# A top-32 attention with a routed feed-forward behind it, on one core: three weight loads set behind the loads of the rest's tokens, and the first expert's second product in four pieces over 512 columns of one bank

## The chip, the cores and the metric

The kernel runs on one NeuronCore of a Trainium2 chip. The metric is the device time of one launch in microseconds; a kernel's figure is the median of its runs. The engines are TensorE (PE, with its weight loads as PEld), VectorE (DVE), ScalarE (ACT), GpSimd (POOL) and SyncE (SP), which does little but issue DMAs.

## The reference

`q`, `k`, `v` are float32, 2 x 8 heads x 576 x 64. Each row of scores keeps its 32 largest, the softmax is taken over these alone, and the result is multiplied with `v`. The output, laid out as 1,152 tokens x 512, goes through a layer of 8 experts with one expert per token:

```python
logits = x @ w_gate;  expert_idx = np.argmax(logits, axis=1)
# gate_w: the softmax value of the chosen expert
# a token takes the next free slot of its expert (288 slots each), in the order of the tokens
h = np.maximum(np.einsum('ecd,edf->ecf', disp, w1), 0.0)   # 512 -> 1024
y = np.einsum('ecf,efd->ecd', h, w2)                       # 1024 -> 512
out[i] = gate_w[i] * y[expert_idx[i], pos[i]]
```

## The kernel before, in words

**Attention.** `attention` walks over 36 units, each one tile of 128 tokens and one pair of heads (`L` is the last unit, 35), in a software pipeline written out by hand. Behind every fourth unit a token tile is finished (`T` is the last of nine tiles, 8) and goes through `route` (L493) in numbered stages: transposes of the attention's output, the logits with `wg` (L525), the largest of eight on DVE, a slot number, and at stage 5.5 an indirect DMA from POOL (L559) that scatters the tile's 128 tokens as rows into `xbuf` in DRAM, by expert and slot. For the last two tiles most of these stages run on DVE.

**Experts.** Every product is done in split precision: a weight comes as float32 (`load_w`, L594, four loads of 1 MB for each expert: two of `w1`, two of `w2`), and `split_w` (L606) makes a half-precision part of it on ACT (L612) and the remainder on DVE (L618); three products of 16-bit parts replace one in float32. The experts are taken in an order that is picked from running counts. From the first picked expert the first 128 tokens (called `a`) are computed inside the attention's last units, from the second one the first 128 tokens (`b`) in the attention's tail. What those two experts have left, 64 + 64 tokens, is "the rest" (`r`): `load_rest` (L644) reads them from `xbuf` with two transposing DMAs (L648), which have to wait until the last tile's scatter has landed, and `ffn_rest` (L763) computes them, its first product at L773 and its second at L761. Then `experts` runs the six other experts from `ffn` (L819), the next one's weights being split meanwhile. The sixteen-bit tokens of expert 2 and 3 come with `load_x` (L632).

**What sets the order here.** All these DMAs except the scatters are issued by SP, in program order: SP waits at the first one whose buffer or data isn't ready, and all later ones stand behind it. The scatters are issued by POOL on a queue of its own. Buffers come from rotating pools; expert 3's weights go to four buffers (`raw`) that exist from the attention's end on. PSUM has eight banks; `tail_p` (L482) names four of them `TAIL_P[0]` to `TAIL_P[3]` for the tail, `bank1` (L83) hands out two others (`pT`) in turn, which the transposed probabilities use too.

**The tail, and the lines that the change touches.** The second product for `a` is cut into four quarters of 128 output columns (`quarter`, L722), each of 24 matmuls (L757) into a `pT` bank, followed by its own copy on ACT (L720); the quarters stand between the last units' steps, and behind the fourth POOL scatters the 128 finished rows to `out` (L677). Then `b`'s first product (L657), the scatter of the last tile, `check` and `count` (a one-column matmul, counts and ranks, L1003 and L1019), and `b`'s second product (L757, with all 512 columns). On SP stand, in this order: the second half of expert 2's `w2` and both halves of expert 3's `w1` (three loads), `load_rest`, expert 2's tokens, both halves of expert 3's `w2`, expert 3's tokens.

Of the kernel before, what the change touches and what calls it, by code (L numbers as in the profile page):

```python
# [34 lines left out]
def kernel(  # L35
# [47 lines left out]
    def bank1():  # L83
        if ("pt", 0) in P:
            return P["pt", 0].tile([128, 512], FT, name="pT", bufs=2)
        return P["p3", 0].tile([128, 9, 128], FT, name="p3", bufs=1).rearrange("p a b -> p (a b)")[:, :512]

    def bank4():
        return bank1().rearrange("p (c t) -> p c t", c=4)
# [618 lines left out]
        nc.gpsimd.tensor_scalar(hh, Q["r"], 1.0, 0.0, op0=OP.mult, op1=OP.add)  # L708
        nc.gpsimd.tensor_tensor(out=hl, in0=Q["r"], in1=hh, op=OP.subtract)

    def quarter_y(c, a):
        if a == 0:
            Q["p"] = bank4()
        for k in (0, 1) if a == 0 else (2, 3):
            small_y("a", 0, Q["p"][:, 0], slice(128 * c, 128 * c + 128), k < 2, k % 2)

    def quarter_out(c):
        if c == 0:
            Q["y"] = work.tile([128, Dm], FT, name="y", tag="nat", bufs=4)
        nc.scalar.activation(Q["y"][:, 128 * c:128 * c + 128], Q["p"][:, 0], AF.Copy, scale=XE["a"][:, 0, 0:1])  # L720

    def quarter(c):  # L722
        quarter_y(c, 0)
        quarter_y(c, 1)
        quarter_out(c)

    def quarter_scatter():
        scatter_y(Q["y"], XE["a"][:, 0, 1:2])

    def small_h(x, e, *fs, first=None):  # L730
        for f in fs:
            g, a = divmod(f, 4)
            if a == 0:
                PA[x, g] = first if first is not None else bank().rearrange("p (c t) -> p c t", c=4) if BANKS else \
                    bank4()
            h_of(PA[x, g][:, a], e, f, x)
# [15 lines left out]
    def small_y(x, e, o, cols, high, g):  # L752
        for i in range(4 * g, 4 * g + 4):
            for lo in range(1 + high):
                fl = dict(start=(high and i == 0 and lo == 0), stop=(not high and i == KF - 1))
                if x != "r":
                    nc.tensor.matmul(o, HA[x][1 - high][:, i], weight(e, 1, lo)(i, cols), **fl)  # L757
                    continue
                for j in range(2):
                    s = slice(64 * j, 64 * j + 64)  # L760
                    nc.tensor.matmul(o[s], HA[x][1 - high][:, i, s], weight(j, 1, lo)(i, cols), **fl)  # L761
# [237 lines left out]

    def check(step):  # L1000
        if step == 1:
            pf = bank1()
            nc.tensor.matmul(pf[:1, 0:1], onesb[:, 0:1], fl[:, 0:1], start=True, stop=True)  # L1003
            nc.vector.tensor_copy(flags[:, 0:1], pf[:1, 0:1])
            return
        ck = work.tile([128, 4, NT * H], FT, name="ck", tag="hl2", bufs=2)
        nc.vector.tensor_scalar(ck[:, 0], CNT, 0.5, None, op0=OP.mult)
        nc.vector.tensor_copy(ci, ck[:, 0])
        nc.vector.tensor_copy(ck[:, 1], ci)
        nc.vector.tensor_tensor(out=ck[:, 2], in0=ck[:, 0], in1=ck[:, 1], op=OP.not_equal)  # L1010
        nc.vector.scalar_tensor_tensor(ck[:, 1], CNT, float(2 * TOPK - S), ck[:, 2], op0=OP.is_lt, op1=OP.add)
        nc.vector.scalar_tensor_tensor(ck[:, 2], CNT, float(2 * TOPK - S + 14), ck[:, 1], op0=OP.is_gt, op1=OP.add)
        nc.vector.tensor_reduce(out=ck[:, 3, 0:1], in_=ck[:, 2], axis=mybir.AxisListType.X, op=OP.max)
        nc.vector.tensor_copy(fl[:, 0:1], ck[:, 3, 0:1])


    def count():
        pc = bank1()
        nc.tensor.matmul(pc[:1, :E], onesb[:, 0:1], OHS, start=True, stop=True)  # L1019
        m = work.tile([1, 4, E, E], FT, name="cm", tag="hl2", bufs=2)  # L1020
        g = m[:, 3]
        n, key, rank = g[:, 0], g[:, 1], g[:, 2]
        down, across = [1, E, E], (lambda a: a[:, None, :].to_broadcast([1, E, E]))
        nc.vector.tensor_copy(n, pc[:1, :E])
        nc.vector.scalar_tensor_tensor(key, n, float(E), last, op0=OP.mult, op1=OP.add)
        nc.vector.tensor_tensor(out=m[:, 0], in0=across(key), in1=key[:, :, None].to_broadcast(down), op=OP.is_gt)
        nc.vector.tensor_reduce(out=rank, in_=m[:, 0], axis=mybir.AxisListType.X, op=OP.add)
        nc.vector.tensor_tensor(out=m[:, 1], in0=across(rank), in1=places[:, :, None].to_broadcast(down),
                                op=OP.is_equal)
        nc.vector.tensor_tensor(out=m[:, 2], in0=m[:, 1], in1=across(e_f[:1]), op=OP.mult)  # L1030
        nc.vector.tensor_reduce(out=g[:, 3], in_=m[:, 2], axis=mybir.AxisListType.X, op=OP.add)
        nc.vector.tensor_copy(order, g[:, 3])
        nc.vector.tensor_tensor(out=m[:, 0], in0=m[:, 1], in1=across(n), op=OP.mult)
        nc.vector.tensor_reduce(out=key, in_=m[:, 0], axis=mybir.AxisListType.X, op=OP.add)
        nc.vector.tensor_tensor(out=n, in0=key, in1=room, op=OP.is_gt)
        nc.vector.tensor_reduce(out=rank[:, 0:1], in_=n, axis=mybir.AxisListType.X, op=OP.max)
        nc.vector.tensor_copy(many, rank[:, 0:1])
        nc.vector.tensor_tensor(out=bad, in0=rank[:, 0:1], in1=flags, op=OP.add)
# [8 lines left out]
    def attention(side, early, late, mid, pads, act, pool, end):  # L1047
# [110 lines left out]
            bound(L, st)  # L1158
        sign(L)
        run(rt(T - 2, 4))  # L1160
        quarter(0)
        values(L - 2)
        seq(select, L - 1, steps=(0, 1, 2, 3))
        run(rt(T - 2, 5))
# [19 lines left out]
        load_w(2, 1, 0)  # L1184
        for st in range(2, 9):
            pick(3, st)
        quarter(1)
        probs(L, 0, 1, 2)
        values(L - 1)
        run(rt(T - 1, 3, 3.5))  # L1190
# [1 line left out]
            split_w(1, 1, 1, half, nc.scalar, 2)  # L1192
        run(rt(T - 1, 4, 5, 5.5))
        split_w(1, 1, 1, 0, nc.vector, 1)
        quarter(2)
        run(rt(T, 0, 0.5))
        values(L)
        run(rt(T, 1))
        quarter(3)
        quarter_scatter()  # L1200
        seq(normalise, L, steps=(0, 1, 2))
        split_w(1, 1, 1, 1, nc.vector, 1)
        load_w(2, 1, 1)
        close_pool("att")
        open_pool("exp")
        for g in range(2):
            load_w(3, 0, g, True)
        run(rt(T, 0.1))
        small_h("b", 1, 0, first=TAIL_P[2].rearrange("p (c t) -> p c t", c=4))
        run(rt(T, 0.6, 1.1, 1.5))  # L1210
        small_h("b", 1, 1)
        run(rt(T, 2.1, 2.2, 3))
        small_h("b", 1, 2)
        run(rt(T, 3.5, 4, 5, 5.5))
        for f in range(3, KF):
            small_h("b", 1, f)
            if f % 4 == 3:
                small_high("b", f // 4)
        check(0)
        check(1)  # L1220
        count()
        load_rest([nc.sync.value_load(row[:, e:e + 1], min_val=0, max_val=(E - 1) * cap + 128) for e in range(2)])
        load_x(2, 0, SIZES[2])
        for g in range(2):
            load_w(3, 1, g, True)
        load_x(3, 0, SIZES[3])
        small_low("b", 0)
        small_low("b", 1)
        split(2, 0, 2)
        split(2, 0, 1)  # L1230
        split(2, 1, 2)
        o = bank1()
        for high in (True, False):
            for g in range(2):
                small_y("b", 1, o, slice(0, Dm), high, g)
# [180 lines left out]
```

## Time and profile before

| | us |
|---|---|
| median of 3 runs (lowest, highest) | 365.16 (362.47, 365.77) |
| the profiled execution | 364.38 |
| its span, first to last instruction | 362.6 |
| PE busy in it | 319.3 (88%) |
| DVE, ACT, POOL busy | 305.5, 283.2, 238.9 |
| DMA traffic | 60.25 MB, mean 166 GB/s |
| mean granted TensorE clock | 0.978 of 2.4 GHz |

Engine times are sums over all instructions, and overlap; a PE that is busy is not a PE at its peak. The attention fills the first 248 us or so, the six experts from `ffn` the last 85, and between them lies the stretch that the change rearranges.

### The profile page before, as it was taken

To read this page: it belongs to the slowest core of one execution; us is meant where nothing else is said; L and a number is where in the kernel's file an instruction comes from. 1 tells how busy PE (TensorE), PEld (TensorE's weight loads), DVE (VectorE), ACT (ScalarE), POOL (GpSimd) and SP (SyncE) were. 2 spreads that over 40 slices of the span, in tenths; PEclk is the share of its full clock that TensorE was granted. 3 is DMA by queue.
4 is the path that set the end of the run, shared out by engine and by line. 5 is a ranking of instruction groups with operands and counts; after the bars stand their busy time and mean duration, and the time that the engine had idled before them with its cause. 6 is when DMAs were issued, how large, how long until landed. Compare 5 with 4: busy or idle time off the path is not lost. (4 is left out here: it accounts for less than half of the span.)

```text
span 362.6 us, 9845 instructions
## 1 busy us (share of the span) xinstructions
PE 319.3 (88%) x3378; PEld 264.9 (73%) x3381; DVE 305.5 (84%) x1605; ACT 283.2 (78%) x498; POOL 238.9 (66%) x274
## 2 busy tenths in 40 slices
PE   6747888898888988989789999989789999999991
PEld 3535776787777876868588888989346999996681
DVE  5879999999999999999999996596626859799940
ACT  5879999999989999899899996762336847786820
POOL 3967979699894998999999989974011010219421
PEclk9888999999999999999899999999989999999998
DMA  9749897964485800000304524527579999997100
GB/s 168 129 106 208 201 217 211 221 150 101 100 281 193 309 3 31 4 0 32 116 3 129 200 82 125 216 98 247 214 213 343 316 392 308 322 381 169 59 25 24
DMA packets 69922, 60.25 MB, mean 166 GB/s; under 512 B 52070, under 2 KB 52070, under 8 KB 69864
## 3 DMA queue, kind: packets, MB, share of 16 engines
q1 hardware_dynamic: 67719, 54.79, 54.7%
q0 software_dynamic: 1616, 4.73, 3.6%
q8 instruction: 28, 0.46, 0.5%
q14 instruction: 31, 0.25, 0.2%
q10 hardware_dynamic: 528, 0.02, 0.1%
HBM read 40.66 MB, written 12.09 MB: 145 GB/s over the span
## 5 line engine op out<-in xcount | busy, mean ns | idle before, releaser
L310 DVE MAX8 un<-s 128x8 f32<-128x72 f32 (+2 forms) x576 | 102.1, 225 | 1.8 <-PE s L292 1.8
L372 POOL TENSOR_TENSOR z<-sm,sg 128x576 f32<-128x576 f32 x71 | 89.4, 1280 | 12.7 <-ACT sg L365 10.6
L677 POOL DMA_INDIRECT out_dram<-y,xp x12 | 24.4, 2033 | 82.8 <-DVE y L853 40.2
L453 PEld LDWEIGHTS pV<-vm,pT 128*128 128x128 f32 (+1 forms) x640 | 72.2, 183 | 6.9 <-issue 3.6
L453 PE MATMUL pV<-vm,pT 128*128 128x65 f32 (+1 forms) x640 | 73.3, 263 | 0.0
L618 DVE TENSOR_TENSOR ws<-wr,ws 128x1024 bf16<-128x1024 f32 x52 | 61.2, 1226 | 2.6 <-ACT ws L612 2.5
L356 ACT ACTIVATE sm<-s,mx 128x576 f32<-128x576 f32 (+2 forms) x108 | 54.7, 580 | 7.3 <-DVE mx L313 7.0
L365 ACT ACTIVATE sg<-sm,mx 128x576 bf16<-128x576 f32 x72 | 55.2, 770 | 5.8 <-POOL z L372 2.7
L292 PE MATMUL s<-qk 128*128 128x512 f16 (+3 forms) x320 | 45.4, 300 | 9.8 <-ACT sm L356 9.8
L428 PE MATMUL p<-ident,sm 128*128 128x128 f32 x252 | 48.3, 281 | 6.0 <-ACT xT L522 5.5
L409 ACT ACTIVATE pen<-sm,nk 128x576 bf16<-128x576 f32 x71 | 51.5, 775 | 1.8 <-DVE nk L400 1.3
L396 DVE MAX8 z<-z 128x8 f32<-128x576 f32 x72 | 51.0, 748 | 1.9 <-POOL z L372 1.9
L612 ACT ACTIVATE ws<-wr 128x2048 f16<-128x2048 f32 (+1 forms) x26 | 47.6, 1840 | 5.7 <-issue 4.4
L657 PEld LDWEIGHTS <-ws 128*128 128x128 f16 (+1 forms) x768 | 48.8, 98 | 0.9 <-issue 0.4
L429 PE MATMUL p<-identB,pen 128*128 128x128 bf16 x252 | 44.6, 220 | 3.5 <-ACT pen L409 3.4
L428 PEld LDWEIGHTS p<-ident,sm 128*128 128x128 f32 x252 | 36.1, 143 | 10.3 <-ACT xT L522 6.8
L429 PEld LDWEIGHTS <-pen 128*128 128x128 bf16 x324 | 33.5, 105 | 6.9 <-ACT pen L409 6.0
L292 PEld LDWEIGHTS <-qk 128*128 128x128 f16 (+1 forms) x320 | 20.8, 107 | 21.7 <-issue 13.8
L430 ACT ACTIVATE pT<-p 128x1152 f32<-128x1152 f32 x28 | 31.9, 1140 | 0.0
L618 POOL TENSOR_TENSOR ws<-wr,ws 128x1024 bf16<-128x1024 f32 x12 | 25.6, 2131 | 0.0
L838 PEld LDWEIGHTS <-ws 128*128 128x128 f16 (+1 forms) x288 | 21.3, 98 | 0.0
L657 PE MATMUL bk<-xe,ws 128*128 128x128 f16 (+7 forms) x312 | 21.1, 227 | 0.0
(276 smaller groups left out, 622.4 us busy)
## 6 DMA issues: line engine op xcount, KB each, us to landing
wr<-in_moe_w_dram SPq DMA_DIRECT2D x32, 1024.0 KB, 6.1
xbuf<-zero SPq DMA_DIRECT2D x6, 771.0 KB, 5.8
qnat<-in_q_dram SPq DMA_DIRECT2D x16, 144.0 KB, 3.5
knat<-in_k_dram SPq DMA_DIRECT2D x16, 144.0 KB, 3.4
out_dram<-zero SPq DMA_DIRECT2D x3, 768.0 KB, 4.6
vm<-in_v_dram SPq DMA_DIRECT2D x16, 128.0 KB, 3.1
qk<-qk SPq DMA_DIRECT2D x14, 144.0 KB, 2.4
vt<-in_v_dram SPq DMA_DIRECT2D x4, 64.0 KB, 4.6
```

Of the source, the lines that this page charges most:

```text
L292: nc.tensor.matmul(PS[u][a][row:row + n, o:o + w], QK[b][2 * i][:, h, s:s + n], QK[b][1][:, h, c:c + w], start=(i == 0), stop=(i == 1))
L310: nc.vector.max(out=un[:, j, i], in_=segment(u, j, i))
L356: nc.scalar.activation(SM[u][:, j, o], i, AF.Identity, bias=VAL[u][0][:, 0, j:j + 1], scale=-1.0)
L365: nc.scalar.activation(SG[u][j], SM[u][:, j], AF.Sign, bias=VAL[u][0][:, 2, j:j + 1], scale=-(1.0 - 2.0 ** -20), accum_out=CNT[:, c:c + 1])
L372: engs[j].tensor_tensor(out=Z[u][:, j], in0=SM[u][:, j], in1=SG[u][j], op=OP.mult)
L396: nc.vector.max(out=z8[:, step - 1], in_=Z[u][:, step - 1])
L409: eng.activation(o, x, AF.Relu, bias=n)
L428: nc.tensor.matmul(pt[:, i], sm[:, cs], ident, start=True, stop=False, is_transpose=True)
L429: nc.tensor.matmul(pt[:, i], pen[:, cs], identB, start=False, stop=True)
L453: nc.tensor.matmul(PV[t][row:row + n, h0 + half], PT[u][:, 5 * half + c, row:row + n], VM[b][:, c, p, half], start=False, stop=(half == 1 ...
L618: eng.tensor_tensor(out=w[:, 1].bitcast(BF)[:, s], in0=r[:, s], in1=w[:, 0, s], op=OP.subtract)
L657: nc.tensor.matmul(o, a(i), c(i), start=(i == 0 and m == 0), stop=(i == k - 1 and m == 2))
```

## The change

Two things. First, on SP three loads of 1 MB (the second half of expert 2's `w2`, both halves of expert 3's `w1`) move from ahead of `load_rest` to behind it, and `load_rest` itself is written ahead of `check` and `count`. Second, `a`'s second product is cut by its terms instead of its columns: the first two pieces hold 8 matmuls each (the half-precision part of the hidden values times both parts of the weights), the last two 4 each, all over 512 columns in one bank, `TAIL_P[2]`; one copy on ACT follows instead of four, and the scatter of those rows is issued behind that of the last tile. For this `b`'s first product now writes `pT` banks, `check` and `count` `TAIL_P[0]`, and `b`'s second product `TAIL_P[3]` (the bank that prints as `ex`).

```diff
@@ -708,21 +708,12 @@
         nc.gpsimd.tensor_scalar(hh, Q["r"], 1.0, 0.0, op0=OP.mult, op1=OP.add)
         nc.gpsimd.tensor_tensor(out=hl, in0=Q["r"], in1=hh, op=OP.subtract)
 
-    def quarter_y(c, a):
-        if a == 0:
-            Q["p"] = bank4()
-        for k in (0, 1) if a == 0 else (2, 3):
-            small_y("a", 0, Q["p"][:, 0], slice(128 * c, 128 * c + 128), k < 2, k % 2)
-
-    def quarter_out(c):
-        if c == 0:
-            Q["y"] = work.tile([128, Dm], FT, name="y", tag="nat", bufs=4)
-        nc.scalar.activation(Q["y"][:, 128 * c:128 * c + 128], Q["p"][:, 0], AF.Copy, scale=XE["a"][:, 0, 0:1])
-
-    def quarter(c):
-        quarter_y(c, 0)
-        quarter_y(c, 1)
-        quarter_out(c)
+    def quarter_y(c):
+        small_y("a", 0, TAIL_P[2], slice(0, Dm), c < 2, c % 2)
+
+    def quarter_out():
+        Q["y"] = work.tile([128, Dm], FT, name="y", tag="nat", bufs=4)
+        nc.scalar.activation(Q["y"], TAIL_P[2], AF.Copy, scale=XE["a"][:, 0, 0:1])
 
     def quarter_scatter():
         scatter_y(Q["y"], XE["a"][:, 0, 1:2])
@@ -999,7 +990,7 @@
 
     def check(step):
         if step == 1:
-            pf = bank1()
+            pf = TAIL_P[0]
             nc.tensor.matmul(pf[:1, 0:1], onesb[:, 0:1], fl[:, 0:1], start=True, stop=True)
             nc.vector.tensor_copy(flags[:, 0:1], pf[:1, 0:1])
             return
@@ -1015,7 +1006,7 @@
 
 
     def count():
-        pc = bank1()
+        pc = TAIL_P[0] if TAIL_P else bank1()
         nc.tensor.matmul(pc[:1, :E], onesb[:, 0:1], OHS, start=True, stop=True)
         m = work.tile([1, 4, E, E], FT, name="cm", tag="hl2", bufs=2)
         g = m[:, 3]
@@ -1158,7 +1149,7 @@
             bound(L, st)
         sign(L)
         run(rt(T - 2, 4))
-        quarter(0)
+        quarter_y(0)
         values(L - 2)
         seq(select, L - 1, steps=(0, 1, 2, 3))
         run(rt(T - 2, 5))
@@ -1184,7 +1175,7 @@
         load_w(2, 1, 0)
         for st in range(2, 9):
             pick(3, st)
-        quarter(1)
+        quarter_y(1)
         probs(L, 0, 1, 2)
         values(L - 1)
         run(rt(T - 1, 3, 3.5))
@@ -1192,44 +1183,43 @@
             split_w(1, 1, 1, half, nc.scalar, 2)
         run(rt(T - 1, 4, 5, 5.5))
         split_w(1, 1, 1, 0, nc.vector, 1)
-        quarter(2)
+        quarter_y(2)
         run(rt(T, 0, 0.5))
         values(L)
         run(rt(T, 1))
-        quarter(3)
-        quarter_scatter()
+        quarter_y(3)
+        quarter_out()
         seq(normalise, L, steps=(0, 1, 2))
         split_w(1, 1, 1, 1, nc.vector, 1)
-        load_w(2, 1, 1)
         close_pool("att")
         open_pool("exp")
-        for g in range(2):
-            load_w(3, 0, g, True)
         run(rt(T, 0.1))
-        small_h("b", 1, 0, first=TAIL_P[2].rearrange("p (c t) -> p c t", c=4))
+        small_h("b", 1, 0)
         run(rt(T, 0.6, 1.1, 1.5))
         small_h("b", 1, 1)
         run(rt(T, 2.1, 2.2, 3))
         small_h("b", 1, 2)
         run(rt(T, 3.5, 4, 5, 5.5))
+        quarter_scatter()
         for f in range(3, KF):
             small_h("b", 1, f)
             if f % 4 == 3:
                 small_high("b", f // 4)
+        load_rest([nc.sync.value_load(row[:, e:e + 1], min_val=0, max_val=(E - 1) * cap + 128) for e in range(2)])
+        load_w(2, 1, 1)
+        load_x(2, 0, SIZES[2])
+        for g in range(4):
+            load_w(3, g // 2, g % 2, True)
+        load_x(3, 0, SIZES[3])
         check(0)
         check(1)
         count()
-        load_rest([nc.sync.value_load(row[:, e:e + 1], min_val=0, max_val=(E - 1) * cap + 128) for e in range(2)])
-        load_x(2, 0, SIZES[2])
-        for g in range(2):
-            load_w(3, 1, g, True)
-        load_x(3, 0, SIZES[3])
         small_low("b", 0)
         small_low("b", 1)
         split(2, 0, 2)
         split(2, 0, 1)
         split(2, 1, 2)
-        o = bank1()
+        o = TAIL_P[3]
         for high in (True, False):
             for g in range(2):
                 small_y("b", 1, o, slice(0, Dm), high, g)
```

The queue of SP around `load_rest` (`wr` is a weight piece, `xe` and `xp` tokens and their scales; the address computations between the rows are left out). Before:

```order
L603 DMA wr_4979<-in_moe_w2_dram 128x4x512
L603 DMA wr_4985<-in_moe_w1_dram 128x2x1024
L603 DMA wr_4987<-in_moe_w1_dram 128x2x1024
L1222 TENSOR_LOAD row_146
L648 DMA_TRANSPOSE xe_5164<-xbuf 128x8x64
L651 DMA xp_5165<-xbuf 64x2
L640 DMA_TRANSPOSE xe_5170<-xbuf 128x8x192
L642 DMA xp_5171<-xbuf 96x2x2
L603 DMA wr_5174<-in_moe_w2_dram 128x4x512
L603 DMA wr_5176<-in_moe_w2_dram 128x4x512
L640 DMA_TRANSPOSE xe_5178<-xbuf 128x8x176
```

Now:

```order
L1208 TENSOR_LOAD row_146
L648 DMA_TRANSPOSE xe_5051<-xbuf 128x8x64
L651 DMA xp_5052<-xbuf 64x2
L603 DMA wr_5057<-in_moe_w2_dram 128x4x512
L640 DMA_TRANSPOSE xe_5059<-xbuf 128x8x192
L642 DMA xp_5060<-xbuf 96x2x2
L603 DMA wr_5063<-in_moe_w1_dram 128x2x1024
L603 DMA wr_5065<-in_moe_w1_dram 128x2x1024
L603 DMA wr_5067<-in_moe_w2_dram 128x4x512
L603 DMA wr_5069<-in_moe_w2_dram 128x4x512
L640 DMA_TRANSPOSE xe_5071<-xbuf 128x8x176
```

The three loads that stood first (4979, 4985, 4987) are 5057, 5063 and 5065 now: one behind the rest's tokens, two behind expert 2's tokens. The rows of L648 and L651 stand twice each.

ACT at the end of the attention (`y` is the result for `a`, `xT` the last tile's transposed output, in two halves). Before:

```order
L612 ACTIVATE ws<-wr 128x1024 x2
L720 ACTIVATE y<-pT,xp 128x128
L522 ACTIVATE xT<-bk 128x256
L720 ACTIVATE y<-pT,xp 128x128
L522 ACTIVATE xT<-bk 128x256
L531 ACTIVATE xs<-xr 128x512
```

Now:

```order
L612 ACTIVATE ws<-wr 128x1024 x2
L522 ACTIVATE xT<-bk 128x256
L716 ACTIVATE y<-bk,xp 128x512
L522 ACTIVATE xT<-bk 128x256
L531 ACTIVATE xs<-xr 128x512
```

The third and fourth copy of 128 columns (the first two stand further ahead) give way to one of 512, in the fourth one's place.

## Rows read from the trace of the kernel before

**Rows 1.** Waits of PE from 225 us on: total us, times, longest.
```profile
PE bk L773 <- DMA xe<-xbuf: 2.3, 2, 1.4
PE pV L450 <- ACT pT L430: 0.7, 1, 0.7
```
**Rows 2.** Timeline of PE: start, us, line, out<-in, count [idle before <-releaser].
```profile
246.86 1.05 PE L757 MATMUL pT<-ws,hh 128*128 128x128 f16 x16
...
248.19 0.39 PE L516 MATMUL bk<-ident,xr 128*128 128x128 f32 x2
...
255.76 3.62 PE L757 MATMUL pT<-ws,hh 128*128 128x512 f16 x15 [0.34 <-DVE cm L1024]
259.21 1.89 PE L757 MATMUL pT<-ws,hl 128*128 128x512 f16 x8
...
262.46 0.40 PE L773 MATMUL bk<-ws,xe 128*64 128x512 f16 x1 [1.36 <-DMA xe<-xbuf]
263.83 7.05 PE L773 MATMUL bk<-ws,xe 128*64 128x512 f16 x47 [0.97 <-DMA xe<-xbuf]
270.82 0.66 PE L780 MATMUL bk<-ident,hs 128*128 128x128 f32 x4
...
274.44 1.92 PE L761 MATMUL pT<-ws,hh 128*64 128x512 f16 x16 [0.37 <-ACT hh L782]
276.19 1.89 PE L761 MATMUL pT<-ws,hl 128*64 128x512 f16 x16
```
**Rows 3.** Busy time by stretch: window, us, engines busy, granted clock, DMA share, GB/s.
```profile
255.00:257.00 2.00, 1.37 (x7) 0.61 (x7) 1.48 (x8) 2.00 (x2) 0.00 (x0) 1.00 1.00 410
264.76:268.17 3.41, 3.41 (x20) 1.42 (x18) 1.29 (x2) 0.00 (x0) 1.01 (x1) 0.50 0.73 150
266.00:333.00 67.00, 66.48 (x808) 57.96 (x805) 50.30 (x57) 45.01 (x49) 13.00 (x6) 0.98 1.07 329
332.00:334.00 2.00, 2.00 (x16) 1.06 (x15) 2.00 (x3) 0.10 (x1) 2.00 (x1) 1.00 0.18 32
```
**Rows 4.** Timeline of SP and its longest wait.
```profile
246.63 1.66 SPq L603 DMA_DIRECT2D wr<-in_moe_w_dram  x3
259.71 2.57 SPq L648 DMA_TRANSPOSE xe<-xbuf  x2
...
264.36 1.44 SPq L640 DMA_TRANSPOSE xe<-xbuf  x1
...
SPq L648 <- DMA xbuf<-xs,ru: 10.0, 1, 10.0
```
**Rows 5.** Timeline of POOL: scatters of the first expert's rows and the last tile's tokens.
```profile
249.04 0.98 POOL L677 DMA_INDIRECT out_dram<-y,xp  x1 [2.82 <-ACT xT L522]
...
252.96 1.00 POOL L559 DMA_INDIRECT xbuf<-xs,ru  x1 [1.66 <-DVE ck L1009]
```
**Rows 6.** Landing of the eight earlier L559 scatters: issue to landing.
```profile
DMA to landing us min/median/max: 3.0/3.1/3.4
```
**Rows 7.** DMA queues (packets, MB, share): 249.04 to 252.9, 253 to 256.9, 257 to 259.
```profile
q1 hardware_dynamic: 580, 1.42, 95.2%
...
q1 hardware_dynamic: 340, 1.33, 83.9%
q0 software_dynamic: 80, 0.26, 16.6%
...
q0 software_dynamic: 79, 0.26, 33.4%
```
**Rows 8.** Timeline of ACT: copies at the attention's end, and the last expert's weights.
```profile
248.40 0.37 ACT L720 ACTIVATE y<-pT,xp 128x128 f32<-128x128 f32 x1 [3.30 <-PE pT L757]
...
263.56 0.67 ACT L1237 ACTIVATE y<-pT,xp 128x512 f32<-128x512 f32 x1
...
340.84 1.92 ACT L612 ACTIVATE ws<-wr 128x2048 f16<-128x2048 f32 x1
344.67 0.69 ACT L815 ACTIVATE y<-bk,xp 128x512 f32<-128x512 f32 x1 [1.92 <-PE bk L757]
```

## The prediction

> **What bounds the kernel now.** I read the waits of PE first. From 225 us to the end PE's longest wait by far is that of the rest's first product (L773) for its tokens, 2.3 us in two pieces [rows 1]; the last row of that view in time is the 0.37 us ahead of 274.44 [rows 2], and behind it PE doesn't wait once. So what this change can give lies before that point, and a microsecond that PE gains there counts to the end unless something else has become late. The timeline of PE [rows 2] shows the place: `b`'s second product ends at about 261.1, the first matmul on the rest starts at 262.46, the second at 263.83, and the 48 last until 270.82. The stretches [rows 3] show what follows from the pause: from 264.76 to 268.17 the granted clock is 0.50 (1.2 instead of 2.4 GHz), where it was 1.00 ahead of the pause. The wait, then, is paid twice, and the stretch from 261.1 to 270.82, 9.7 us, holds 48 matmuls that need far less.
>
> Why the tokens are late is seen on three queues. SP issues the three weight loads at 246.63 to 248.29 and then waits 10.0 us for the last scatter [rows 4]. POOL issues that scatter at 252.96 [rows 5], and SP comes through at 259.71: 6.75 us, where the eight earlier ones landed after 3.0 to 3.4 [rows 6]. In between the three loads pass: the hardware queue holds the DMA engines for 95% of the time until 252.9, and the software queue moves nothing, though the scatter of `a`'s rows was issued at 249.04. That one's 80 packets go through by 256.9, the tokens' 79 only from 257 to 259 [rows 5, 7]. I read that as scatters kept back by the weights.
>
> **The tokens.** With the three loads behind `load_rest`, nothing of weight size is under way when the scatter is issued. I take the median landing of the eight, 3.1 us [rows 6]; the bounds are 3.0 and the 6.75 of now. That brings SP's transposes to 3.65 us earlier by itself.
>
> The trace says that the scatters were kept back until the loads were nearly through [rows 7]. The Trainium skill ("DMA: Bandwidth & Descriptors", Queues, rings and completion order) says otherwise: each DMA engine takes turns between the queues it has work for, packet by packet. By that rule the tokens lose little to the loads, and the whole change would bring 1.4 us instead of the 5.5 of the sum; the packets of rows 7 speak against it.
>
> **The four pieces.** A quarter now takes 248.19 - 246.86 = 1.33 us for 24 matmuls of 128 columns; the other three look the same. Over 512 columns with the same kind of weights, 16 take 259.21 - 255.76 = 3.45 us, 0.216 each [rows 2]. So the pieces take 8 x 0.216 = 1.72, 1.72, 0.86 and 0.86 us: the first two 0.39 longer, the last two 0.47 shorter. The first two lie ahead of the place where PE waits 0.7 us for ACT's exponentials at L450 [rows 1]; I cost them at nothing, with that wait as their cover (without it, 0.8 us). The last two lie behind it, in the chain from the last unit to the last tile's route, so PE reaches the last transposes (L516, 248.19) 0.94 us sooner. On ACT the copy of `a` still stands ahead of the tile's `xT`: 0.67 us for 512 columns (L1237) [rows 8] in place of the fourth quarter's 0.37, so 0.30 of it is given back; the three other copies go, where ACT had room. Net 0.64. All that comes then hangs on this chain: logits, slots, the scatter of the tokens, `b`'s first product.
>
> **Other banks and moves.** `count` no longer shares a bank with `b`'s second product, and the wait of 0.34 us for DVE at 255.76 goes [rows 2]. That product then starts at 255.76 - 0.64 - 0.34 = 254.8 and ends at about 260.1. The scatter of `a`'s rows moves behind that of the tokens on POOL; it costs POOL 0.98 us [rows 5] at a time when POOL has nothing else, and nobody reads `out`. `load_rest` ahead of `check` changes nothing on SP, since neither issues there.
>
> **The sum.** Scatter at 252.96 - 0.64 = 252.3; landing 3.1 later; SP's first transpose at 255.5 instead of 259.71, 4.2 us sooner; the second half of the tokens is usable 263.83 - 259.71 = 4.12 us behind that, at 259.6, ahead of PE's 260.1. Both waits go, by half a microsecond only. Without the pause the clock should stay: 16 such matmuls take 276.19 - 274.44 = 1.75 us at full clock [rows 2], so 48 take 5.25 and end at 265.35 instead of 270.82. That is 5.5 us: 1.0 ahead of the product, 2.3 of waits, and the remaining 2.2 mostly the 3.4 us at half clock (1.7) and the matmul that ran alone. 364.38 (the profiled execution) becomes 358.9; it stands 0.8 below the median of the runs, so **the forecast is 365.16 - 5.5 = 359.7 us**.
>
> **What is late next: the weights.** From 266 to 333 the DMA engines have no rest (share 1.07, which counts overlapping packets, 329 GB/s); only at 332 to 334 does it fall to 0.18 [rows 3]. Three loads of 1.05 MB that used to pass before 259 now enter this stretch. At 410 GB/s each costs 2.6 us, at 329 it costs 3.2, so 7.7 to 9.6. The stretch starts sooner: the first of them stands where expert 2's tokens were issued, 264.36 [rows 4], less 4.2. All loads behind come 3.5 to 5.4 us later while PE wants them 5.5 sooner: 9.0 to 10.9 us of slack are used. The last weight piece is in by some 332.4 (the share of the last row) and is taken by ACT at 340.84, and ACT idles 1.92 us behind it [rows 8]: 8.4 + 1.9 = 10.3. That covers all but the far end, so I cost this at nothing, and at 0.6 us for the upper bound. Earlier pieces have more room.
>
> **Rivals.** (1) *The queues share fairly*, and the scatter is slow for another reason. The tokens' 79 packets are 5 for each of 16 engines; a weight packet let in ahead of each holds 1.33 MB / 340 = 3.9 KB [rows 7] and takes 0.15 us at a sixteenth of 410 GB/s: 0.8 us in all. The second half then arrives at 263.83 - 0.64 - 0.8 = 262.4, PE waits 2.3 us as before and the clock falls: 365.16 - 1.4 = 363.8. For it speaks only that both queues did move packets between 253 and 256.9. Chance 0.10.
>
> (2) *The tokens come sooner, but the clock falls all the same*, or a wait of a microsecond is left (the margin is 0.5). Half of 3.41 us is 1.7: 361.4. The clock was at 1.00 from 255 to 257, and the pause is all that lies between. Chance 0.15.
>
> (3) *Slower: the weights become the bound.* The place is ACT's split of the last expert's fourth piece (340.84), the price each microsecond by which it lands behind 340.84 + 1.92. If the scatter stays at 6.75 us, the head start is 0.64 instead of 4.2; with loads at 329 GB/s the last piece lands at 332.4 + 9.6 - 0.6 = 341.4, still covered. It decides from 342.8 on: 1.4 us more, which three more loads in a saturated queue can cost, as can a second pause of PE with its 1.7 us of half clock. I take 3 us beyond cover and pause: 368. Against it stands that the loads fit in by rate. Chance 0.05.
>
> (4) *No effect*, the moved loads being late on another path that takes back all that is won: 365. Chance 0.03.
>
> **The numbers.** The forecast has 0.67; with the runs' spread (362.47 to 365.77) its own range is 358 to 361.3. A change of 1% (3.65 us) is about what a measurement of this kernel tells from none. Faster by more than that, below 361.5: all of the forecast and half of rival 2, 0.74. Within: the other half, rivals 1 and 4 and part of 3, 0.21. Slower: 0.05. The range goes from 357.6 to 363.2: it takes in rival 2 and leaves out 1, 3 and 4.
>
> **What will show it.** In the new profile the last L559 lands some 3 us after its issue; SP's L648 starts near 255.5; no wait for `xe` at the rest's first product, whose 48 matmuls take 5.2 to 5.4 us at a granted clock of 1.00; the copy of `a` is one of about 0.67 us. The forecast is wrong if SP's wait for the scatter lasts as long with the engines idle, if a stretch at half clock is left, or if ACT's L612 of the last experts waits for a load.

## The result, and the profile after

The change made the kernel faster by 1.3%: 359.93 us (359.45 to 360.11) against 364.94 us (362.47 to 365.77) in the same series, ratio 0.9874 [0.9839, 0.9909]. A second series of both gave 360.21 and 365.04 us, 0.9874 [0.9828, 0.9919]. (One execution of 1,734.61 us is left out of the first figures; none like it came again in six more runs of the same kernel, and its cause is open.) The forecast was 359.7 us. The profiled execution took 359.45 us with a span of 357.7, where it was 364.38 and 362.6.

Line numbers behind the change are lower than before, most by 9: `b`'s second product is L748, the rest's first product L764 and its transposes L771, the second product of an expert's 128 tokens L748 too; the copy of `a`, inside the change, is L716. The experiments that start from the kernel before keep its numbers (in e5 those behind the added line are one higher).

I read the scatter first, on POOL's timeline of the changed kernel, with its landing from the DMA issues (line, operation, count, median us to landing):

```profile
252.17 1.01 POOL L559 DMA_INDIRECT xbuf<-xs,ru  x1 [2.17 <-DVE ck L1000]
253.49 0.98 POOL L677 DMA_INDIRECT out_dram<-y,xp  x1 [0.30 <-issue]
```
```profile
xbuf<-xs,ru POOLq DMA_INDIRECT x1, 3.1
```

It is issued 0.79 us sooner than before and lands after 3.1 us where it took 6.75 [rows 4, 5]. SP's timeline answers to it:

```profile
255.30 2.56 SPq L648 DMA_TRANSPOSE xe<-xbuf  x2
...
259.59 0.41 SPq L603 DMA_DIRECT2D wr<-in_moe_w_dram  x1
260.20 2.30 SPq L640 DMA_TRANSPOSE xe<-xbuf  x1
...
263.73 3.01 SPq L603 DMA_DIRECT2D wr<-in_moe_w_dram  x4
```

SP passes at 255.30 instead of 259.71 [rows 4], and the three loads follow behind. Next PE's timeline, at the same places as in [rows 2], and one place near the end:

```profile
246.23 1.02 PE L748 MATMUL bk<-ws,hl 128*128 128x512 f16 x4
247.09 0.38 PE L516 MATMUL bk<-ident,xr 128*128 128x128 f32 x2
...
254.57 3.63 PE L748 MATMUL ex<-ws,hh 128*128 128x512 f16 x16
258.07 1.90 PE L748 MATMUL ex<-ws,hl 128*128 128x512 f16 x8
259.91 5.37 PE L764 MATMUL bk<-ws,xe 128*64 128x512 f16 x48
265.21 0.66 PE L771 MATMUL bk<-ident,hs 128*128 128x128 f32 x4
...
336.06 1.90 PE L748 MATMUL bk<-ws,hh 128*128 128x512 f16 x8 [0.73 <-ACT hh L732]
```

The last transposes of the attention come at 247.09 instead of 248.19. The rest's 48 matmuls stand in one row with no idle time ahead of it, and end at 265.2 where they ended at 270.82: 5.61 us won here. The stretches (columns as in [rows 3]) show the clock:

```profile
264.76:268.17 3.41, 3.28 (x30) 1.68 (x26) 1.20 (x2) 2.83 (x3) 0.23 (x1) 1.00 1.14 179
261.00:333.00 72.00, 71.53 (x906) 63.15 (x903) 57.68 (x62) 51.78 (x55) 20.47 (x8) 1.00 1.08 339
332.00:334.00 2.00, 2.00 (x30) 1.64 (x28) 1.70 (x2) 1.77 (x3) 1.70 (x2) 1.00 1.04 384
```

The granted clock is 1.00 where it was 0.50. The third row shows the price: at 332 to 334 the DMA share is 1.04 and not 0.18, so the weights now arrive some microseconds later, and PE wants them sooner. The waits of PE from 225 us on, and ACT's timeline, show where that bites:

```profile
PE pV L450 <- DVE xr L469: 1.0, 1, 1.0
PE bk L748 <- ACT hh L732: 0.7, 1, 0.7
PE pV L450 <- ACT pT L430: 0.7, 1, 0.7
```
```profile
247.29 0.69 ACT L716 ACTIVATE y<-bk,xp 128x512 f32<-128x512 f32 x1 [2.81 <-PE bk L748]
...
330.98 1.91 ACT L612 ACTIVATE ws<-wr 128x2048 f16<-128x2048 f32 x1 [0.26 <-DMA wr<-in_moe_w_dram]
333.61 1.91 ACT L612 ACTIVATE ws<-wr 128x2048 f16<-128x2048 f32 x1 [0.23 <-DMA wr<-in_moe_w_dram]
335.42 0.58 ACT L732 ACTIVATE hh<-pV 128x512 f16<-128x512 f32 x1
336.87 1.91 ACT L612 ACTIVATE ws<-wr 128x2048 f16<-128x2048 f32 x1 [0.86 <-DMA wr<-in_moe_w_dram]
339.72 0.69 ACT L806 ACTIVATE y<-bk,xp 128x512 f32<-128x512 f32 x1 [0.94 <-PE bk L748]
```

Of the last expert's four weight pieces ACT waits for three. The third one's split ends at 335.5, the `hh` (hidden values) that stand behind it on ACT come late, and PE idles 0.73 us at 336.06. The fourth piece is the latest, by 0.86 us, yet costs PE nothing: behind its split ACT idles 0.94 us until PE is done. The two ends meet: 5.61 - 0.73 = 4.88 us, and the span is 4.9 shorter.

### The profile page after: what moved, and what is told of

The parts are those of the page before. It is cut to its first block, busy times and chain, and to the rows that moved or that the text cites. A ratio compares the mean times of both kernels' runs of the same rounds, so it can differ in the third digit from the quotient of the medians.

```text
span 357.7 us, 9700 instructions
## 1 busy us (share of the span) xinstructions
PE 315.1 (88%) x3309; PEld 259.9 (73%) x3309; DVE 305.5 (85%) x1605; ACT 282.5 (79%) x495; POOL 239.5 (67%) x274
## 5 line engine op out<-in xcount | busy, mean ns | idle before, releaser
L372 POOL TENSOR_TENSOR z<-sm,sg 128x576 f32<-128x576 f32 x71 | 89.4, 1279 | 13.1 <-ACT sg L365 10.9
L453 PEld LDWEIGHTS pV<-vm,pT 128*128 128x128 f32 (+1 forms) x640 | 71.3, 181 | 6.7 <-issue 3.3
L453 PE MATMUL pV<-vm,pT 128*128 128x65 f32 (+1 forms) x640 | 72.4, 261 | 0.0
L292 PE MATMUL s<-qk 128*128 128x512 f16 (+3 forms) x320 | 43.4, 292 | 8.8 <-ACT sm L356 8.8
L657 PE MATMUL pT<-xe,ws 128*128 128x128 f16 (+2 forms) x336 | 21.4, 221 | 0.4 <-ACT pen L409 0.4
```

Source lines behind the costliest of these rows:

```text
L292: nc.tensor.matmul(PS[u][a][row:row + n, o:o + w], QK[b][2 * i][:, h, s:s + n], QK[b][1][:, h, c:c + w], start=(i == 0), stop=(i == 1))
L372: engs[j].tensor_tensor(out=Z[u][:, j], in0=SM[u][:, j], in1=SG[u][j], op=OP.mult)
L453: nc.tensor.matmul(PV[t][row:row + n, h0 + half], PT[u][:, 5 * half + c, row:row + n], VM[b][:, c, p, half], start=False, stop=(half == 1 ...
L657: nc.tensor.matmul(o, a(i), c(i), start=(i == 0 and m == 0), stop=(i == k - 1 and m == 2))
```

## The experiments

All kernels of one series share their runs of the kernel before; its median was 365.04 in the first series (the first four kernels), 364.85 in the second, 363.7 in the third. "Ahead" counts the 1 MB loads that stand ahead of `load_rest` on SP, "order" says whether the scatter of `a`'s rows is issued behind that of the tokens, "lands" is the tokens' scatter from issue to landing. A wait marked PEld is that of a weight load in the middle of the 48 matmuls for the second half of the tokens; it isn't among PE's own waits, but makes the 48 take longer.

| | ahead | order | pieces | lands | PE's wait for `xe` | the 48 matmuls | us | ratio to before |
|---|---|---|---|---|---|---|---|---|
| before | 3 | no | no | 6.75 | 2.3 | 0.40 + 7.05 | 365.0 | 1 |
| after_again | 0 | yes | yes | 3.1 | none | 5.37 | 360.21 | 0.9874 [0.9828, 0.9919] |
| e1_loads_only | 0 | no | no | 4.2 | 0.2 (PEld) | 5.67 | 363.09 | 0.9957 [0.9913, 1.0001] |
| e2_pieces_only | 3 | yes | yes | 6.1 | 2.0 | 0.40 + 7.05 | 364.0 | 0.9962 [0.9932, 0.9992] |
| e3_one_ahead | 1 | yes | yes | 3.0 | none | 5.37 | 359.46 | 0.9853 [0.9808, 0.9898] |
| e4_two_ahead | 2 | yes | yes | 4.2 | 0.4 (PEld) | 5.90 | 359.65 | 0.9878 [0.9833, 0.9924] |
| e5_warm_in_pause | 3 | no | no | 6.9 | filled, 0.2 (PEld) | 5.66 | 363.05 | 0.9972 [0.9942, 1.0001] |
| e6_one_ahead_no_pieces | 1 | no | no | 4.5 | 0.4 (PEld) | 5.87 | 360.19 | 0.9896 [0.9851, 0.9942] |
| e7_scatter_order_only | 3 | yes | no | 6.3 | 1.8 | 0.40 + 5.37 | 363.3 | 0.998 [0.9943, 1.0016] |
| e8_five_ahead | 5 | yes | yes | 7.4 | 6.0 | 8.53 | 368.38 | 1.0126 [1.0084, 1.0167] |
| e9_no_pieces_scatter_behind | 1 | yes | no | 3.8 | none | 5.37 | 360.23 | 0.9904 [0.9864, 0.9943] |

**The changed kernel once more.** Expected:

> The changed kernel once more, beside the others of this chip. Theory (the three loads kept the scatter of the last tokens back, and PE's pause brought half clock): 359.9 us again, the rest's first product without a wait, and a wait of 0.7 us at the last expert but one (L748 for hh) because its successor's weights land late. One earlier execution of six took 1,734.6 us; if that belongs to the kernel it comes again in some execution here, if it was the chip's it does not.

Measured 360.21, with the 0.7 us wait of PE for `hh` again.

**The loads alone.** The kernel before, and on SP:

```diff
-        load_w(2, 1, 1)
...
-        for g in range(2):
-            load_w(3, 0, g, True)
...
+        load_rest([...])
+        load_w(2, 1, 1)
+        load_x(2, 0, SIZES[2])
+        for g in range(4):
+            load_w(3, g // 2, g % 2, True)
+        load_x(3, 0, SIZES[3])
         check(0)
         check(1)
         count()
-        load_rest([...])
-        load_x(2, 0, SIZES[2])
-        for g in range(2):
-            load_w(3, 1, g, True)
-        load_x(3, 0, SIZES[3])
```

> The three loads behind load_rest, the quarters and the banks as before. Theory: the scatter (issued near 253.0) lands in 3.0 to 3.4 us, SP's transposes start near 256.2 instead of 259.7, the second half is usable near 260.3, ahead of PE's 261.1, the clock stays at 1.00 and the 48 matmuls take 5.3 us: 4.4 us less ahead of the experts, some 0.2 of it lost to late weights, 360.7. Rival (the queues share the engines fairly, the gain comes from the pieces): the scatter still takes over 6 us, both waits stay, 364.9.

Measured 363.09, with an interval that just reaches 1 and runs that spread from 360.60 to 367.96. PE's timeline, at the rest and near the end, and SP's at the four loads behind:

```profile
261.03 5.67 PE L773 MATMUL bk<-ws,xe 128*64 128x512 f16 x48
...
339.10 1.90 PE L757 MATMUL bk<-ws,hh 128*128 128x512 f16 x8 [2.11 <-ACT hh L741]
```
```profile
266.00 2.31 SPq L603 DMA_DIRECT2D wr<-in_moe_w_dram  x4
```

PE has no pause, and the transposes start at 266.62, 4.2 us sooner than before. But the scatter landed after 4.2 us, where 3.0 to 3.4 was expected, so SP passed at 257.24 and not near 256.2; and 2.11 us are lost at the late weights, where 0.2 was expected. The second miss hangs in part on the first, since the loads stand behind the tokens on SP: the four are issued at 266.00 where the changed kernel has 263.73, 2.3 us later, while PE's transposes are only 1.4 us later (266.62 and 265.21). By this account 0.9 us of the 1.4 by which the wait exceeds the changed kernel's 0.73 come from the late tokens; the rest isn't explained.

**The pieces alone.** The changed kernel with the three loads ahead again, and `load_rest` behind `check` and `count` again:

```diff
+        load_w(2, 1, 1)
         close_pool("att")
         open_pool("exp")
+        for g in range(2):
+            load_w(3, 0, g, True)
...
-        load_rest([...])
-        load_w(2, 1, 1)
-        load_x(2, 0, SIZES[2])
-        for g in range(4):
-            load_w(3, g // 2, g % 2, True)
-        load_x(3, 0, SIZES[3])
         check(0)
         check(1)
         count()
+        load_rest([...])
+        load_x(2, 0, SIZES[2])
+        for g in range(2):
+            load_w(3, 1, g, True)
+        load_x(3, 0, SIZES[3])
```

> The four pieces, the banks and the later scatter of the first expert's rows, with the three loads where they were. Theory: the loads end at 258.6 whatever PE does, so the tokens' scatter lands as late as before although it is issued 0.7 us sooner; PE comes 1.0 us earlier to the same wait, pauses 3.3 to 3.7 us, the clock falls: 364.9, no gain. Rival (fair queues): the scatter lands 0.7 us sooner with its issue: 364.2; rival (the pieces and the later scatter of the first expert's rows are what counts): 362 or less.

Measured 364.0. PE's timeline and one stretch:

```profile
260.10 0.40 PE L764 MATMUL bk<-ws,xe 128*64 128x512 f16 x1 [1.00 <-DMA xe<-xbuf]
261.50 7.05 PE L764 MATMUL bk<-ws,xe 128*64 128x512 f16 x47 [1.01 <-DMA xe<-xbuf]
```
```profile
262.00:265.00 3.00, 3.00 (x16) 1.29 (x14) 2.36 (x2) 0.57 (x1) 1.26 (x1) 0.50 0.59 123
```

The wait and the half clock are both still there: with the loads ahead the pieces bring about 1 us and no more. The median is the fair queues' number (364.2) rather than the theory's (364.9), and as that rival had it the scatter lands sooner with its issue. But it also lands after 6.1 us where it took 6.75, which neither has. What both lacked is the order of the two scatters (e7 below).

**One load back ahead.** The changed kernel with one line moved:

```diff
+        load_w(2, 1, 1)
         close_pool("att")
...
         load_rest([...])
-        load_w(2, 1, 1)
```

> As the changed kernel, but the first of the three loads (second half of expert 2's w2) goes back ahead of load_rest. Theory: that load is through at 251.6, before the scatter's issue at 252.2, so the rest's tokens come as in the changed kernel (SP near 255.3); all later weights come 2.6 us sooner, and the 0.7 us wait of PE near the end goes: 359.2. Rival (the late wait is ACT's own and has nothing to do with the loads): 359.9. Rival (any load ahead costs): 361 or more.

Measured 359.46, the lowest median here; in the same series the changed kernel has 360.21, and the runs of the two overlap (358.94 to 361.03 and 359.61 to 361.84). PE's timeline:

```profile
260.15 5.37 PE L764 MATMUL bk<-ws,xe 128*64 128x512 f16 x48
```

One load ahead keeps nothing back: SP passes at 255.47, and PE doesn't wait for the tokens. The 0.7 us at the late weights is gone.

**Two loads back ahead.** As above, with `load_w(3, 0, 0, True)` ahead as well.

> The changed kernel with two of the three loads back ahead of the rest's tokens (the second half of expert 2's w2 and the first half of expert 3's w1); only one load stays behind. A dose between the kernel with one load ahead (scatter landed 3.05 us after its issue, SP's first L648 at 255.5, 359.5 us) and the one with all three ahead (6.1 us, 364.0). Theory (the last tile's scatter does not start until the loads that were queued ahead of it are nearly through, so its delay is that of the last queued byte): two loads of 1.05 MB issued at about 245.5 and 247 leave the engines near 252.5 to 253, so the scatter, issued about 252.3, lands at 256 to 256.7, PE waits 0.5 to 1.2 us for xe at the rest's first product, a stretch at half clock may follow, 360.3 to 362. Rival (the scatter is late in proportion to the bytes ahead of it, two thirds of 3 us): lands 257.5, PE waits 1.5 to 2, half clock, 362 to 363. Rival (queues share fairly and the loads matter little): lands 255.5, as in the changed kernel, 359.5.

Measured 359.65. The scatter, issued at 252.17, lands 4.2 us later. The DMA queues (packets, MB, share of 16 engines) in two windows, 252.17 to 254 and 254 to 255:

```profile
q1 hardware_dynamic: 159, 0.61, 81.2%
q0 software_dynamic: 17, 0.07, 9.6%
...
q0 software_dynamic: 58, 0.18, 44.6%
q1 hardware_dynamic: 9, 0.02, 7.7%
```

Most of the scatter's packets (the software queue) go through when the two loads are nearly out. The changed kernel's scatter, issued at 252.17 too, had moved 26 packets by 254 (window 251 to 254):

```profile
q0 software_dynamic: 26, 0.11, 9.0%
```

With 17 packets against 26 this scatter isn't kept back; it shares the engines with the end of the loads. SP passes at 256.39, as the theory had it. The cost was expected too high (360.3 to 362): PE reaches the rest's product at 259.90 and its 48 matmuls take 5.90 instead of 5.37, so only 0.5 us is lost and no clock. The weight load's wait (waits of PEld):

```profile
PEld L764 <- DMA xe<-xbuf: 0.4, 1, 0.4
```

**A busy PE in the pause.** The kernel before with twelve matmuls added that nobody reads:

```diff
+        warm(12)
         take_banks()
         ffn_rest(side(1))
```

> The kernel before with twelve added matmuls of 512 columns on a bank that nobody reads, written between b's second product and the rest's first product, so that PE is busy in the pause of 2.3 us in which it waits for the tokens. The wait itself stays. Theory (the pause is what makes the granted clock fall): no stretch at 0.50 behind it, the rest's 48 matmuls take 5.3 to 5.5 us instead of 7.05 plus the single one of 0.40, and 1.7 us are won: 363.3. Rival (the clock falls for another reason, or the 48 matmuls are slow because of their operands): the stretch at 0.50 stays and the time is 365, or more if the added matmuls delay the real ones.

Measured 363.05, with an interval that just reaches 1. PE's timeline (L1046 is the added work) and the stretch that was at 0.50 [rows 3]:

```profile
260.74 2.75 PE L1046 MATMUL bk<-onesb,identb 128*128 128x512 bf16 x12
263.42 5.66 PE L773 MATMUL bk<-ws,xe 128*64 128x512 f16 x48
269.01 0.66 PE L780 MATMUL bk<-ident,hs 128*128 128x128 f32 x4
```
```profile
264.76:268.17 3.41, 3.41 (x35) 1.81 (x32) 1.09 (x1) 0.60 (x1) 0.81 (x1) 1.00 0.74 153
```

The tokens come as late as before, yet the transposes start at 269.01 instead of 270.82. Of these 1.81 us 0.2 are an earlier start of everything (the last eight matmuls of `b`'s second product stand at 259.01, and at 259.21 in [rows 2]); 1.6 are won by work that is thrown away. With the pause filled the clock did not fall, so in these two profiles the fall hangs on the pause, and it cost about the 1.7 us that the prediction put on it. That every such pause brings it isn't shown (e7 below).

**One load ahead, without the pieces.** The edit of the loads alone, but `load_w(2, 1, 1)` stays where it was.

> The kernel before with only the loads moved, and of these only two: both halves of expert 3's w1 behind the rest's tokens, the second half of expert 2's w2 left ahead of them; load_rest written ahead of check and count; the first expert's second product and its scatter untouched. With all three moved, the same kernel had 363.1 us: the tokens' scatter landed 4.2 us after its issue, no wait for xe and no half clock, but 2.1 us lost at the last experts' weights. Theory (the weights' loads that enter behind are what costs 2.1 us there, so with one load less behind, the loss goes as it went in the kernel with the pieces): scatter lands 4.2 to 4.6 us after 252.9, no wait at L757 for late weights above 0.7, 361.2. Rival (the loss at the end comes from somewhere else than the number of loads behind): 363.

Measured 360.19, 1.0 us better than the theory asked for. ACT waits for none of the last expert's weights, and the 2.11 us of e1 is gone with one load of 1.05 MB, which takes 3.1 us at the 337 GB/s of this kernel's stretch from 262 to 333. The number of loads behind is what costs there.

**The order of the two scatters alone.** The kernel before, `quarter_scatter()` moved from behind `quarter(3)` to behind `run(rt(T, 3.5, 4, 5, 5.5))`.

> The kernel before with one thing alone: the scatter of a's rows (L677) issued on POOL behind that of the last tile's tokens, where it stood 3.9 us ahead of it. All three loads stay ahead. Theory (in the software queue the tokens' packets stood behind the 64 packets of a's rows, which themselves waited for the loads; that is the 0.8 us by which the tokens came sooner in the kernel with the pieces alone): the scatter, issued about 252.9, lands 5.5 to 6.3 us later instead of 6.75, PE's wait for xe falls from 2.3 to 1.5 to 1.9 us, the half clock stays, 364.4. Rival (the order of the two scatters does not matter, only the loads do): landing 6.7, 365.0. Rival (the scatter starts as soon as it is first in its queue, sharing with the loads): landing 4 us, no wait, 361.

Measured 363.3, with an interval that reaches past 1. PE's timeline and the stretch of the 47 matmuls:

```profile
262.46 0.40 PE L773 MATMUL bk<-ws,xe 128*64 128x512 f16 x1 [0.80 <-DMA xe<-xbuf]
263.90 5.37 PE L773 MATMUL bk<-ws,xe 128*64 128x512 f16 x47 [1.04 <-DMA xe<-xbuf]
```
```profile
263.90:269.20 5.30, 5.30 (x47) 2.63 (x48) 2.36 (x2) 1.50 (x3) 1.26 (x1) 1.00 0.68 123
```

The scatter lands 6.3 us after its issue instead of 6.75, so the order is worth half a microsecond and the loads the rest. What wasn't expected: with waits of 0.80 and 1.04 us the clock did not fall, where e2's 1.00 and 1.01 made it fall. One profile each doesn't settle why.

**Five loads ahead.** The pieces alone, with both halves of expert 3's `w2` moved ahead too (the loop over two halves becomes one over four).

> The kernel with the pieces alone (all three loads ahead of the rest's tokens as before; its scatter landed 6.1 us after its issue, its packets began 3.3 us after it, 364.0 us), with both halves of expert 3's w2 moved ahead as well: five loads of 1.05 MB ahead instead of three, some 5.2 us of transfers more at 400 GB/s. Theory as the prediction had it (the scatter is kept back until the loads queued ahead of it are nearly through): its packets begin some 8.5 us after its issue and it lands 11 to 11.5 us after it, SP's first L648 at 262.5 or later, PE waits about 7 us for xe with the clock falling: 367.5 to 369. Rival (a scatter is kept back by what is already under way, up to some 4 us, and then shares the engines with the loads behind: the scatter of a's rows in the kernel before began 4.2 us after its issue with 4.7 us of weights still to come): packets begin 3.3 to 4.2 us after the issue and the last lands 6.5 to 7.5 after it, PE waits 2 to 3.5 us: 364 to 365.5.

Measured 368.38: the theory's time, but a scatter that is nearer the rival's. The DMA queues in three windows, 252.26 (the issue) to 257, 257 to 260, 260 to 263:

```profile
q1 hardware_dynamic: 477, 1.72, 99.9%
...
q1 hardware_dynamic: 326, 0.67, 58.8%
q0 software_dynamic: 159, 0.53, 45.0%
...
q1 hardware_dynamic: 608, 1.20, 104.8%
```

For 4.7 us after its issue the scatter moves nothing, a little more than the rival's 3.3 to 4.2 and far from the theory's 8.5. Then both scatters go through beside the weights, which fill the engines for another 3 us. The tokens' one lands at 7.4 us, not at 11. What makes PE wait 6.0 us is the next link (PE's timeline and a stretch in it):

```profile
266.07 8.53 PE L764 MATMUL bk<-ws,xe 128*64 128x512 f16 x48 [6.01 <-DMA xe<-xbuf]
```
```profile
266.07:271.50 5.43, 5.31 (x23) 2.09 (x25) 0.00 (x0) 0.00 (x0) 0.00 (x0) 0.50 0.81 187
```

SP issues the first transpose at 259.67, as in the kernel before, but the tokens are usable 6.4 us later, where it was 262.46 - 259.71 = 2.75 [rows 2, 4]: the transposes are issued by SP like the weights, on their queue, which has the engines at 104.8% until 263. And 5.4 us and more go at half clock.

**The pieces' own worth.** The kernel e6 with the scatter of `a`'s rows behind the tokens' one, as in e7.

> The kernel with two of the three loads behind and without the pieces (360.2 us; the tokens' scatter landed 4.5 us after its issue at 252.78), and in addition the scatter of a's rows issued behind the tokens' one. Against the same with the pieces and count's own bank (359.5) this leaves only these out, which the prediction took for 0.64 + 0.34 = 1.0 us in the chain to b's second product. Theory: scatter at 252.8 to 253.3, landing 3.1 us later, SP's first L648 near 256.1, the rest's 48 matmuls begin at 260.9 (b's second product is the bound) without a wait and take 5.4: 360.0, so 0.5 to 1.0 above the kernel with the pieces. Rival (the pieces are worth nothing, their time goes elsewhere): 359.5. Rival (the order of the two scatters is what made the difference of 1.4 us in landing; the pieces none): landing 3.1 and 359.5.

Measured 360.23. PE's timeline, to be set beside e3's 260.15:

```profile
261.14 5.37 PE L773 MATMUL bk<-ws,xe 128*64 128x512 f16 x48
```

Without the pieces and the bank the product comes 0.99 us later, against the 0.64 + 0.34 = 0.98 of the sum. The medians, 359.46 and 360.23, are of two series and 0.8 apart. Against e6 (360.19, of another series too) the order of the scatters doesn't show in the median. In the profiles it does: the landing comes down from 4.5 to 3.8 us (3.1 was expected), the weight load's wait of 0.4 us is gone, and the 48 matmuls take 5.37 instead of 5.87.

## Why the prediction was right, and where its steps were off

**The tokens: right in size, half right in mechanism.** Landing 3.1 us, SP at 255.3 (255.5 forecast): as worked out. The reason given was that the scatters "were kept back until the loads were nearly through". The runs show something narrower: the tokens' scatter took 3.0 to 3.1 us with none or one of the three loads ahead and the pieces in, 4.2 with two, 6.1 with three, and 7.4 with five. Behind two it starts as it does behind none (e4). Behind five it is kept back, but for 4.7 us, with weights passing for much longer, and from then on it shares. The scatter of `a`'s rows in the kernel before could have told this: nothing of it moved for the first 3.9 us, and then its 80 packets went through while the weights still held the engines for 84% of the time [rows 5, 7]. So "until the loads were nearly through" was the step that failed, though not in this change, where nothing is left ahead.

For the rest of the way the rule that the prediction set against itself holds. The Trainium skill ("DMA: Bandwidth & Descriptors", Queues, rings and completion order) has each DMA engine take turns between its queues; e8's second window, 326 packets beside 159, is such sharing, though it doesn't show the turns one by one. The same section says that an engine consumes the descriptors of a ring in order, which agrees with e8's transposes at 6.4 instead of 2.75 us behind the weights. The 4.7 us ahead of the first packet are not explained by turns from the moment of issue; rival 1, built on them alone, gave 1.4 us for the whole change, and fell.

**The pieces and the bank: right.** 0.98 us forecast, 0.99 measured between e9 and e3. In the changed kernel `b`'s second product started at 254.57 (254.8 forecast) and ended at 259.9 (260.1), and the copy of `a` took 0.69 us (0.67). Only the cover of the first two pieces was another than forecast: PE's wait of 0.7 us at L450 is still there in full, and the second piece used up a wait of PE for DVE that stood behind it, here before and after:

```profile
238.53 0.23 PE L429 MATMUL pT<-identB,pen 128*128 128x128 bf16 x1 [0.56 <-DVE r L536]
238.38 0.23 PE L429 MATMUL pT<-identB,pen 128*128 128x128 bf16 x1 [0.18 <-DVE pen L411]
```

The first piece cost nothing either: PE starts the piece at 230.05 and the logits behind it (L525) at 233.73, both 0.15 us sooner than before, and a wait of 0.16 us for DVE is gone there. That these two had room was luck, since the prediction had not looked at them.

**The pause and the clock: right.** The wait of 2.3 us is gone, and the 48 matmuls take 5.30 at a granted clock of 1.00 (5.25 forecast). e5 splits the two: 1.6 us were the clock's alone in its profile. Rival 2, the clock falling all the same, did not occur. The margin of half a microsecond was right too. SP's pass and the 4.12 us of the sum put the second half of the tokens at 259.42 in the changed kernel, 0.49 ahead of PE, which lost nothing; in e4 and e6 they put it at 260.51 and 261.44, both 0.6 behind PE's start (259.90 and 260.84), and there the 48 matmuls took 0.53 and 0.50 us longer.

**The weights: mis-sized, at a piece that wasn't looked at.** "I cost this at nothing, and at 0.6 us for the upper bound": it cost 0.73 in the changed kernel. The balance, 9.0 to 10.9 us used of a slack of 10.3, was made for the last expert's fourth piece, and there it held: behind that split ACT idled for PE, 1.92 us before [rows 8] and still 0.94 now, of which PE's own wait gives 0.73. What failed is the sentence behind the balance, "Earlier pieces have more room". The kernel before, on ACT and on PE, at the third piece:

```profile
338.56 1.91 ACT L612 ACTIVATE ws<-wr 128x2048 f16<-128x2048 f32 x1
340.36 0.59 ACT L741 ACTIVATE hh<-pV 128x512 f16<-128x512 f32 x1
```
```profile
339.01 3.90 PE L757 MATMUL bk<-ws,hh 128*128 128x512 f16 x15
```

Behind this split stand the `hh` for the second half of PE's sixteen matmuls (one isn't recorded), which PE reaches half way through them, at about 340.9, just as the `hh` end at 340.95. So nothing idled behind the third piece, where 1.92 us did behind the fourth. Now its split starts at 333.61 instead of 338.56, 4.95 us sooner, and PE comes 5.61 us sooner: 0.66 of the 0.73. The loads passed at 339 GB/s (the stretch from 261 to 333 above), 3.1 us for each, between the two prices in the sum. e1 shows the same debt at 2.11 us, e3 and e6 show none with one load less behind. So rival 3's mechanism, the weights as the next bound, is real, at a quarter of the price that it was given.

**The sum.** 5.5 forecast; 5.61 measured at the rest, less 0.73 at the end, 4.88 in the span. 359.7 against 359.93.

**What stays open.** Why e1 and e6 land their scatter after 4.2 and 4.5 us with no weights queued behind which it could stand; that a few packets of each come half a microsecond and more behind the others (in e1 four of 80 after 256) is seen, not explained. And the runs of the kernel before spread from 362.2 to 366.6 us in the second series, those of e3, e4 and e6 over 0.8 to 2.1 us, of e9 over 3.0 and of e1 over 7.4. e5 has a median 1.8 us below that kernel's, but nearly the same lowest run (361.94 and 362.17), as if the clock fell in some executions of the kernel before and not in others; single runs leave only a mean clock, so this isn't shown.

## What to carry to other kernels

When a small transfer that everything waits for shares the engines with large loads, look at what is queued at the moment of its issue, not at the mean DMA share. Move only as many loads behind it as the wait needs, and count the slack of the loads at every piece, with what idles behind its user: here the third piece was the tight one and not the last. With two of the three loads behind, the profile lost nothing there, and the median was 0.75 us lower than with all three, with runs that overlap. A pause of PE has to be priced with the clock that may fall behind it: here 2.3 us of waiting and 1.6 more.

## What the runs showed of the hardware that was not expected

- A scatter of 128 rows landed after 4.2, 6.1 and 7.4 us behind two, three and five queued loads of 1 MB; behind five it moved nothing for 4.7 us and then shared the engines.
- A transposing DMA on the weights' queue stands behind them: 6.4 us to usable tokens in e8, 2.75 in the kernel before.
- Twelve useless matmuls of 512 columns in a pause of 2.7 us brought the end of the work behind it 1.6 us nearer.
- The granted clock stayed at 1.00 behind waits of 0.80 and 1.04 us, and fell to 0.50 behind 1.00 and 1.01 us, in one profile each.
